# The second tile's attention in quarter steps, and a new order of eight loops: an RWKV-6 and GELU MLP kernel

## Chip, cores and metric

One core of a Trainium2 chip. The metric is the device time of one execution in microseconds (us), the median of three runs. An engine's own time is read from one profiled execution, whose span runs from its first instruction to its last.

## What is computed

The reference, cut to what matters (batch B=4, heads H=8, sequence S=768, head width D=48; the MLP has 3072 rows, 384 columns, 2048 hidden columns):

```python
for t in range(S):
    cur = einsum('bhd,bhe->bhde', u[None] * k[t], v[t])
    y[:, :, t] = einsum('bhd,bhde->bhe', r[t], state + cur)
    state = w[t][..., None] * state + einsum('bhd,bhe->bhde', k[t], v[t])
x = y.transpose(0, 2, 1, 3).reshape(B * S, H * D)
h = x @ w_in
out = (0.5 * h * (1 + erf(h / sqrt(2)))) @ w_out
```

So a linear attention with a decay w per key column and a bonus u for the current step, followed by a GELU MLP over its rows. All data are float32, the weights of the MLP arrive as float64.

## The kernel before

**Tiles and loops.** The 3072 rows are cut into eight tiles of 384 (a half sequence of one batch, all heads). `for x in range(NX)` (L1241) runs eight loops. Loop x interleaves the MLP of tile x-1 (`mlp`, L920) with the attention of tile x (`attention`, L373) and the first steps of the attention of tile x+1. In loop 0 there is no MLP: two halves of tile 0's attention run beside each other. After the last loop comes the MLP of tile 7 alone. The "second tile" is tile 1, whose attention lies in loop 1 (the second loop); the third tile's loop is loop 2.

**Order.** Each part is a Python generator that emits a few instructions and yields. `PLAN[x]` (L38) is a string, one character per step: `.` the MLP (in loop 0 the first half of tile 0's attention), `s` the current tile's attention, `f` the next tile's, `l` loads of the next tile, `c` conversion of weights, `w` masks and sums of weights, `x` sums of x. Every engine takes its instructions in the order in which the strings emit them, and what a string leaves over is emitted at its end. The strings come from a planner with costs of its own, outside the kernel.

**Attention inside a tile.** Time is cut into chunks of 64. Inside a chunk the score matrix (`a_sb`) is built in levels. `halves` (L489) has six levels h = 1, 2, ..., 32: a block of 2h steps is cut in two, PE multiplies the keys of the chunk with the queries of the later halves (`products`, L465, 48 products of 64x64 by 32 columns for tile 1), DVE multiplies r and k in place by the decay across the half (L525), and DVE (L536, by mask) or ACT (L533, by rows, from h=16) copies the result out of PSUM into `a_sb`. `quarters` (L560), which tiles 2 to 7 use, takes steps of four blocks: h=4 covers what levels 4 and 8 do, h=16 what 16 and 32 do, with 48 products of 96 columns (L608). It needs the queries laid out with their decays (ACT L577, DVE L582 and L583), updates r (L662) and k (L669, L673), and copies out by mask on DVE (L641) or by rows on ACT (L624). Levels 1 and 2 of these tiles are done by `transposed_sums` on DVE (L398).

**State.** k is turned: tiles 0 and 1 do it on PE (L705) with a copy on ACT (L707); tiles 2 to 7 by DVE block transposes (L556), twelve DMAs of 32x32 blocks on SP's queue (`move_block`, L551) and four ACT copies (L715). Then come `kv_ps` (L731), the chain of states on DVE (L746), y inside a chunk (L772), y from the states (L817), and the copies to the MLP's input xT (L824, L840, L843 with small DMAs L847).

**Weights.** w_in and w_out are 16 pieces of 768 columns (0 to 7 w_in, 8 to 15 w_out), turned from float64 to float32 by three ACT and three DVE instructions each (`prepare` L350 to L352, `finish` L363, L365, L369). The buffers between ACT and DVE are two deep (`HALFWAY`), the raw ones five (`AHEAD`); the load of piece i+3 is emitted when piece i is finished (L335). `w_sums` (L858) makes three sums of quarters of w_out in eight subtractions (L864) for the MLPs from tile 1 on, which multiply 2x2 blocks with seven products instead of eight. The MLP of tile 0 uses the plain form (L1074, L1168: 16 row blocks of w_out, two products each).

**PSUM.** Up to loop 1 there are three pairs of banks (`pair`) and two single ones (`mm`); after it two pairs and two `u` banks (`fewer_pairs`).

Of the kernel before, what the change touches and what calls it, by code (L numbers as in the profile page):

```python
# [28 lines left out]
LEVELS = (1, 2, 4, 8, 16, 32)  # L29
QUARTERS = (4, 16)  # L30
FINE = 4
# [4 lines left out]
NC_SP = 8  # L36
HALFWAY = 2
PLAN = {  # L38
    0: ".lls.....sslsc.lsslll.sl.sls..sl.lscsl..sss.lscs.lscs.s.clll.s..s.cccsss...wss..ss.ff",
    1: (  # L40
        ".cswc.ccc.cccss.lc.ccscs..cc.cs.cclwcsc.ccssc.c.cccsccc..ssccc.c.lcls.cc.ccsc.w.clwscclccc"
        ".c.swcw.ss.ccs.lcsc..cwcccslccslff..w..fw.wfs..f..flffffffww"
    ),
    2: (
        "...l...s..ws.swssswssss.sslsw...ssss.sssws.ll..ws.w..lw.sw.wl.sls.sls..lf.s....sf..f.f.xx."
        "fxl.x.x"
    ),
    3: (
        "l..sss..s.s..s.s....s...s.ssllss.sss.s.s.ss.l..lsss..ssslss.ss.s..s......s..ls.llssf.sf.sf"
        "lf.f.x.x..xxfffxf"  # L50
    ),
    4: (
        "...s...lsl......s.s....sss..ssss..s..ss..s..s...llssslss....sl.sss...s...sll.sl.s.sfs..fsf"
        ".ff..xl.x.xfffxffx"
    ),
    5: (
        ".l..........ls.ss...s.sslls.ssss..ss.sls...sss..sssssl.ss.s..s.......s.lssll.sfsf.f.s.ff.x"
        "..x.xxxl"
    ),
    6: (  # L60
        "sss.sls.....s......ls.s....s.sssssss..s.....s.ss....s.s.ssss.s.l.ss.l.ls.l...s.l.lslssf.s."
        ".ffs..lff.xx..xffxffx"
    ),
    7: "......s.s....s.s...s.ssssss...sss.ss...sss..ssss.s...ss...s...s.s.ss.s.s.s.x.x...xxx",
}


# [5 lines left out]
def kernel(  # L73
# [232 lines left out]
            nc.gpsimd.tensor_copy(out=v, in_=ident[o, o].unsqueeze(1).to_broadcast([32, FINE, 32]))  # L306

    def make_quarter_masks():
        make_fine()
        yield  # L310
        for (h, a), m_q in m_qs.items():
            nc.vector.tensor_tensor(out=quarter[h][a], in0=s_qs[h][:, 0:m_q.shape[1]], in1=m_q, op=ALU.is_equal)
            yield
# [59 lines left out]
    def attention(x, unit):  # L373
# [114 lines left out]

        def halves():  # L489

            for h in LEVELS:
                m = C // 2 // h
                if np_ < NPART:

                    d = products(range(np_), lambda z, b, i, p: rc[z, b, i, p], C, h == 1)
                    d = d.rearrange("p g (n m two j) -> p g n m two j", two=2, j=h, m=m)[:, :, :, :, 1, :]
                else:
                    right = rc.rearrange("p b i c (m two j) -> p b i c m two j", two=2, j=h)[:, :, :, :, :, 1, :]
                    d = products(range(np_), lambda z, b, i, p: right[z, b, i, p], C // 2)
                    d = d.rearrange("p g (n m j) -> p g n m j", j=h, m=m)  # L500
                if h == 1:
                    yield
                    diag = diagonal()
                yield

                r2 = r.rearrange("p (n two j) -> p n two j", two=2, j=h)[:, :, 1, :]
                t2 = tot[h].rearrange("p (n two) -> p n two", two=2)[:, :, 0:1].to_broadcast(r2.shape)
                k2 = k.rearrange("p (n two j) -> p n two j", two=2, j=h)[:, :, 0, :]
                tk = tot[h].rearrange("p (n two) -> p n two", two=2)[:, :, 1:2].to_broadcast(k2.shape)
                rk = bass.AP(tensor=r2.tensor, offset=r2.offset, ap=[r2.ap[0], [n_u - h, 2]] + list(r2.ap[1:]))  # L510
                tt = bass.AP(tensor=t2.tensor, offset=t2.offset, ap=[t2.ap[0], [1, 2]] + list(t2.ap[1:]))

                def update(z, r2=r2, t2=t2, k2=k2, tk=tk):
                    nc.vector.tensor_mul(*((k2, k2, tk) if z is k else (r2, r2, t2)))

                if x == 0 and m == 1:

                    update(k)
                    last_r.append(lambda: update(r))
                elif x == 0 and h == 1:  # L520
                    update(r)
                    yield
                    update(k)
                else:
                    nc.vector.tensor_mul(rk, rk, tt)  # L525
                yield
                ah = at.rearrange("p g n (m two j) -> p g n m two j", two=2, j=h)[:, :, :, :, 1, :]
                if h >= 16:

                    for p in range(2):  # L530
                        for i in range(m):
                            s = slice(p * 64 + i * 2 * h, p * 64 + i * 2 * h + h)
                            nc.scalar.copy(out=ah[s, :, :, i], in_=d[s, :, :, i])  # L533
                else:
                    mask = masks[h].rearrange("p (m j) -> p m j", j=h).unsqueeze(1).unsqueeze(1)
                    nc.vector.copy_predicated(out=ah, mask=mask.to_broadcast(ah.shape), data=d)  # L536
                if h == 1:
                    copy_diagonal(diag)
                yield
# [20 lines left out]
        def quarters():  # L560
# [28 lines left out]
            for h in QUARTERS:  # L589
                m, r4, t4, s0, s1, s2 = views(h)  # L590

                def burst(first, behind, spare=False):

                    d = [bank_u(i) for i in range(2)] if spare else pair("d")
                    if behind == n_b and h == FINE:
                        for a in range(FINE):
                            for g in range(2):
                                for p in range(2):
                                    nc.tensor.matmul(fine_of(d, g)[half[p], a * n_b:],  # L599
                                                     lhsT=places[half[g], a, p * C:(p + 1) * C],  # L600
                                                     rhs=fine_sb[half[g], 0:FINE - a, a],
                                                     start=(a == 0), stop=True, skip_group_check=True)
# [39 lines left out]
                        o += w_q  # L642

                last = h == QUARTERS[-1]
                whole = last and x % 2 == 0
                cuts = (0, n_b // 3, 2 * n_b // 3, n_b) if whole else (0, 5, 10, n_b)
                parts_of = list(zip(cuts, cuts[1:]))
                ds = [burst(*parts_of[0])]
# [1 line left out]
                    yield  # L650
                ds.append(burst(*parts_of[1]))
                if whole:
                    ds.append(burst(*parts_of[2], spare=True))
                yield
                copy_quarters(*parts_of[0], ds[0])
                yield
# [26 lines left out]
                for z, d in list(zip(parts_of, ds))[1:]:  # L683
                    copy_quarters(*z, d)
                    yield
                if h == FINE:
                    mask = fine_mask.rearrange("p (m b) -> p m b", b=FINE).unsqueeze(1)
                    for g in range(2):
                        data = fine_of(ds[-1], g).rearrange("p (b n) -> p n b", n=n_b)
# [3 lines left out]
                        yield  # L693

        last_r = []
        yield from halves() if x < 2 else quarters()


        if x < 2:
            kts = []  # L700
            for b in range(np_):
                kt_ps = pair("kt_ps")
# [523 lines left out]
    def next_v():  # L1226
        load_v(1, nc.sync)
        yield

    def warm():  # L1230
        for _ in range(2):
            keep_warm(3, True)
            yield

    def masks_and_sums():
        yield from make_quarter_masks()
        yield from w_sums()

    pieces_of_w = weights()
    slots = iter(())  # L1240
    for x in range(NX):  # L1241
# [8 lines left out]
        else:  # L1250
# [1 line left out]
                ".": mlp(x - 1), "s": slots, "f": following,  # L1252
                "l": load(x + 1, nc.sync),
                "x": sums_of_x(x) if x > 1 else iter(()),
                "w": masks_and_sums() if x == 1 else chain(first_sum(), h_sums()) if x == 2 else iter(()),
                "c": pieces_of_w if x == 1 else iter(()),
            }
        for c in PLAN[x]:
# [69 lines left out]
```

## Time and profile before

| What | us |
|---|---|
| Median of three runs (lowest, highest) | 593.21 (592.66, 593.95) |
| The profiled execution, its own time | 593.38 |
| Its span | 591.6 |
| PE busy in the span | 573.7 |
| DVE busy | 453.5 |
| ACT busy | 279.8 |
| First MLP product of tile 0 (L1074) | at 46.0 |
| End of tile 0's w_out products and of tile 1's y (L817) | at 114.8 |
| First MLP product of tile 2 (L949) | at 193.2 |

The profile has, for each instruction, its engine, line, tile names, start and length. A float32 matmul of the program is two records on PE. A wait is put down to what ended last before it. The chain of work is followed back from the last instruction; the table of stretches gives the busy time of each engine in a window.

### The profile page before, as it was taken

How to read it: one execution, taken by the hardware profiler on the slowest of the kernel's cores; microseconds unless marked ns; L12 is line 12 of the kernel's file. 1: busy time of each engine (PE TensorE's matmuls, PEld its weight loads, DVE VectorE, ACT ScalarE, POOL GpSimd, SP SyncE). 2: the span in 40 equal slices, each digit the busy share in tenths (PEclk: the TensorE clock that was granted, in tenths of full speed). 3: DMA queues.
4: the chain of work that ended last, by engine and by line, in shares of the span. 5: the costliest groups of instructions: out<-in, count | busy, mean ns of one | idle time of the engine just before them, and what ended most of it. 6: DMA issues, size and time to landing. Idle time of an engine off the chain costs nothing.

```text
span 591.6 us, 17422 instructions
## 1 busy us (share of the span) xinstructions
PE 573.7 (97%) x7522; PEld 510.8 (86%) x7536; DVE 453.5 (77%) x871; ACT 279.8 (47%) x648; POOL 8.0 (1%) x21
## 2 busy tenths in 40 slices
PE   5779999999999999999999999999999999999998
PEld 3566666766799999999999999999999999999997
DVE  5989989998969986787859987688859998421432
ACT  2367889223612558046462458145560465435400
POOL 3100000000000000000000000000000000000000
DMA  6658581020142302241032311330025200210000
GB/s 237 197 192 308 163 287 56 32 89 2 29 140 78 108 22 35 76 125 38 1 61 84 122 38 21 93 120 2 2 34 160 72 2 8 35 46 0 1 14 33
DMA packets 51004, 46.80 MB, mean 79 GB/s; under 512 B 31728, under 2 KB 36080, under 8 KB 50928
## 3 DMA queue, kind: packets, MB, share of 16 engines
q1 hardware_dynamic: 50832, 45.62, 25.6%
q8 instruction: 59, 0.97, 0.7%
q14 instruction: 17, 0.14, 0.1%
q10 hardware_dynamic: 96, 0.07, 0.1%
HBM read 36.24 MB, written 4.72 MB: 69 GB/s over the span
## 4 chain that ended last, share of the span: by engine, by line
PE 91%; DVE 3%; DMA 2%; issue 1%; ACT 1%; SPq 0%; DVEq 0%; ACTq 0%
PE o_ps L1088 33%; PE h_ps L949 16%; PE u_ps L949 14%; PE h_ps L1074 11%; PE d L608 4%; PE o_ps L1168 4%; PE d L472 2%; PE y_ps L772 2%; PE y_ps L817 2%; PE kv_ps L731 2%; DVE st L746 1%; DMA rkw<-in_rkw_dram 1%; DMA raw<-in_w_in_dram 1%; ACT a_sb L533 1%; PE d L599 1%
## 5 line engine op out<-in xcount | busy, mean ns | idle before, releaser
L949 PE MATMUL h_ps<-xT,w_in_sb 128*128 128x192 f32 x480 | 95.5, 330 | 0.4 <-DVE o_sb L1185 0.4
L949 PEld LDWEIGHTS h_ps<-xT,w_in_sb 128*128 128x128 f32 x480 | 79.7, 190 | 4.0 <-ACT g L981 1.5
L1074 PE MATMUL h_ps<-xT,w_in_sb 128*128 128x384 f32 x192 | 64.2, 490 | 0.1
L1074 PEld LDWEIGHTS h_ps<-xT,w_in_sb 128*128 128x128 f32 x192 | 35.8, 190 | 24.1 <-ACT xT L824 0.4
L1088 PE MATMUL o_ps<-w_out_sb,g 128*128 128x192 f32 x224 | 39.7, 326 | 0.0
L1088 PEld LDWEIGHTS o_ps<-w_out_sb,g 128*128 128x128 f32 x224 | 37.0, 190 | 0.3
L949 PE MATMUL u_ps<-s,w_in_sb 128*128 128x192 f32 x192 | 35.3, 327 | 0.0
L624 ACT COPY a_sb<-d 32x256 f32<-32x256 f32 (+8 forms) x90 | 32.6, 363 | 4.6 <-PE d L608 3.1
L472 PEld LDWEIGHTS d<-rkw 64*64 64x64 f32 x1152 | 19.5, 138 | 15.6 <-issue 10.0
L949 PEld LDWEIGHTS u_ps<-s,w_in_sb 128*128 128x128 f32 x192 | 31.7, 190 | 0.2
L1088 PE MATMUL o_ps<-w_out_sb,f 128*128 128x192 f32 x176 | 31.6, 329 | 0.0
L1088 PE MATMUL o_ps<-t,g 128*128 128x192 f32 x176 | 31.4, 329 | 0.0
L1088 PE MATMUL o_ps<-w_out_sb,e 128*128 128x192 f32 x176 | 31.4, 329 | 0.0
L1088 PE MATMUL o_ps<-t,e 128*128 128x192 f32 x176 | 31.2, 328 | 0.0
L1088 PE MATMUL o_ps<-t,s 128*128 128x192 f32 x176 | 30.9, 327 | 0.0
L746 DVE SCALAR_TENSOR_TENSOR st<-st,tot_sb,kv_ps 128x48 f32<-128x48 f32 x160 | 29.0, 258 | 1.7 <-PE kv_ps L731 1.6
L472 PE MATMUL d<-rkw 64*64 64x64 f32 (+1 forms) x1152 | 22.1, 225 | 8.1 <-DMA rkw<-in_rkw_dram 4.1
L641 DVE COPY_PREDICATED a_sb<-quarter,d 128x480 f32<-128x480 uint8 (+5 forms) x54 | 23.2, 438 | 8.6 <-PE d L608 7.3
L1088 PEld LDWEIGHTS o_ps<-t,g 128*128 128x128 f32 x176 | 28.7, 190 | 0.4
L1088 PEld LDWEIGHTS o_ps<-w_out_sb,e 128*128 128x128 f32 x176 | 28.7, 190 | 0.3
L1088 PEld LDWEIGHTS o_ps<-w_out_sb,f 128*128 128x128 f32 x176 | 28.7, 190 | 0.3
L1088 PEld LDWEIGHTS o_ps<-t,e 128*128 128x128 f32 x176 | 28.8, 190 | 0.2
(165 smaller groups left out, 1134.0 us busy)
## 6 DMA issues: line engine op xcount, KB each, us to landing
rkw<-in_rkw_dram SPq DMA_DIRECT2D x54, 256.0 KB, 3.8
raw<-in_w_out_dram SPq DMA_DIRECT2D x8, 768.0 KB, 4.4
v_in<-in_v_dram SPq DMA_DIRECT2D x8, 584.0 KB, 3.9
raw<-in_w_in_dram SPq DMA_DIRECT2D x5, 768.0 KB, 7.0
out_dram<-o_sb SPq DMA_DIRECT2D x20, 192.0 KB, 2.0
rkw<-kx SPq DMA_DIRECT2D x72, 48.0 KB, 2.1
rkw<-in_rkw_dram SPq DMA_DIRECT2D x6, 384.0 KB, 5.5
raw<-in_w_in_dram SPq DMA_DIRECT2D x9, 256.0 KB, 5.1
```

The costliest lines, as they stand in the source:

```text
L472: nc.tensor.matmul(d[half[p], g, n * width:(n + 1) * width], lhsT=kc[half[g], b, i, p], rhs=right(half[g], b, i, p), start=True, stop=True)
L608: nc.tensor.matmul(o[half[p], i * 3 * C // 2:(i + 1) * 3 * C // 2], lhsT=kc[half[g], n // NI, n % NI, p], rhs=rx[half[g], 2 * n + p], star ...
L624: nc.scalar.copy(out=at[z, g, first:behind, (a + 1) * h:], in_=d[z, :, :, to] if g == slice(None) else d[z, :, to])
L641: nc.vector.copy_predicated(out=an[:, :, :, :, (a + 1) * h:], mask=mask.to_broadcast(data.shape), data=data)
L731: nc.tensor.matmul(kv_ps[half[g], p, i * D:(i + 1) * D], lhsT=k_t(b, i, p, g), rhs=vs(b, i, g)[half[p], 0:D], start=True, stop=True)
L746: nc.vector.scalar_tensor_tensor(out=stq[:, q, c], in0=stq[:, q, c - 1] if c else b4[:, q, NC - 1], scalar=totq[:, q, c:c + 1], in1=kvs[q ...
L772: nc.tensor.matmul(y[p][half[g ^ swap(b)], i * C:(i + 1) * C], lhsT=vs(b, i, g)[half[p]], rhs=at[half[p], g, b * NI + i, :], start=(i == 0 ...
L817: nc.tensor.matmul(ys[b][0][c % 2][half[g ^ swap(b)], i * C:(i + 1) * C], lhsT=src[half[g], o:o + G], rhs=rc[half[g], b, i, c % 2], start= ...
L949: nc.tensor.matmul(o, lhsT=lhsT, rhs=rhs, start=start, stop=True, skip_group_check=True)
L1074: nc.tensor.matmul(h_ps, lhsT=w_in_sb[:, f // FI, j, f % FI * 128:(f % FI + 1) * 128], rhs=xT[:, j, :], start=(j == 0), stop=(j == NJ - 1))
L1088: nc.tensor.matmul(o, lhsT=lhs(j), rhs=rhs(j), start=start and j == 0, stop=(j == HF - 1), skip_group_check=True)
L1168: nc.tensor.matmul(o, lhsT=block(i, f // HF, f % HF), rhs=w_out_sb[:, f, :], start=(f == 0), stop=(f == NF - 1))
```

## The change

- Tile 1's attention does levels 1 and 2 by `halves` and the rest by `quarters` (steps 4 and 16), each step in three parts of four blocks, all on pairs of banks; the fine step of `quarters` stays with tiles 2 to 7. Its k is turned as in tiles 2 to 7 (DVE transposes, twelve DMAs on SP, four ACT copies).
- The quarter masks are made in loop 0 (behind the load of tile 1's v) instead of loop 1; the fine mask stays in loop 1.
- `w_sums` is one generator shared by two loops: four of its eight steps in loop 1, the rest in loop 2.
- All eight strings of `PLAN` are new.

```diff
 PLAN = {
-    0: ".lls.....sslsc.lsslll.sl.sls..sl.lscsl..sss.lscs.lscs.s.clll.s..s.cccsss...wss..ss.ff",
+    0: ".ll.s.s...slls.ssscll.lll..ss.ll.ss.lssl.ssclsc.l.ssslc.ls..sc..s.ss..wwswwccc.ccss.s.ccs.",
     1: (
-        ".cswc.ccc.cccss.lc.ccscs..cc.cs.cclwcsc.ccssc.c.cccsccc..ssccc.c.lcls.cc.ccsc.w.clwscclccc"
-        ".c.swcw.ss.ccs.lcsc..cwcccslccslff..w..fw.wfs..f..flffffffww"
+        "cscss.c..cscsslcc.lsss.ccl.cls.ccscc.ccs.ls.ccs..cclssssscsc.ssswccss..cs.cc.scc.c.cc.cssc"
+        "c.ccc.lscc.c.cwcccclc.lsccccwcc.f..w...fw....f.fffffflf"
     ),
...
     def make_quarter_masks():
-        make_fine()
-        yield
         for (h, a), m_q in m_qs.items():
...
-            for h in LEVELS:
+            for h in LEVELS if x == 0 else LEVELS[:2]:
...
-                    if behind == n_b and h == FINE:
+                    if behind == n_b and h == FINE and x > 1:
...
-                whole = last and x % 2 == 0
+                whole = x == 1 or last and x % 2 == 0
...
-                    ds.append(burst(*parts_of[2], spare=True))
+                    ds.append(burst(*parts_of[2], spare=x > 1))
...
-                if h == FINE:
+                if h == FINE and x > 1:
...
-        yield from halves() if x < 2 else quarters()
-        if x < 2:
+        if x < 2:
+            yield from halves()
+        if x > 0:
+            yield from quarters()
+        if x == 0:
             kts = []
...
     def next_v():
         load_v(1, nc.sync)
         yield
+        yield from make_quarter_masks()
...
+    of_w_out = w_sums()
     def masks_and_sums():
-        yield from make_quarter_masks()
-        yield from w_sums()
+        make_fine()
+        yield
+        yield from islice(of_w_out, 4)
...
-                "w": masks_and_sums() if x == 1 else chain(first_sum(), h_sums()) if x == 2 else iter(()),
+                "w": masks_and_sums() if x == 1 else chain(of_w_out, first_sum(), h_sums()) if x == 2 else iter(()),
```

In the built program the lines behind the change stand one or two apart from before (L1168 is L1169, L731 is L732, L608 is L606, L556 is L554, L551 is L549). On PE, tile 1's 48 products with u now stand ahead of the first three row blocks of the MLP instead of behind the first; in loop 1 the steps are level 1, the products with u, nine MLP products, level 2, nine, step 4, eighteen, step 16, twelve, eight of w_out, kv, four of w_out, y, six, y from the states, fourteen. On DVE, weight pieces 0 and 1 and two thirds of piece 2 stand ahead of the copies to xT (before: piece 0 and two thirds of piece 1), pieces 0 to 10 ahead of the chain of states (before: pieces 0 to 14 and the first instruction of piece 15), and the last piece's last instruction after two sums instead of three. On SP, the twelve DMAs of tile 1 stand ahead of the loads of pieces 11 to 14.

## The prediction

> **What bounds the kernel now.** I read the busy shares first, then the table of stretches, then the chain in order of time, then each engine's timeline around the second loop (tile 0's MLP beside tile 1's attention), which the change rewrites. The busy shares:
>
> ```profile
> PE 573.7 (97%) x7522; PEld 510.8 (86%) x7536; DVE 453.5 (77%) x871; ACT 279.8 (47%) x648; POOL 8.0 (1%) x21
> ```
>
> PE is the bound on average. An average hides stages, so I took stretches of 15 us (columns: PE, PEld, DVE, ACT, POOL, clock, DMA share, GB/s):
>
> ```profile
> 45.00:60.00 15.00, 14.95 (x230) 9.40 (x229) 14.71 (x22) 11.77 (x24) 0.00 (x0) 1.00 0.86 302
> 60.00:75.00 15.00, 15.00 (x163) 9.10 (x163) 14.90 (x18) 12.84 (x24) 0.00 (x0) 1.00 0.54 168
> 75.00:90.00 15.00, 15.00 (x218) 9.73 (x211) 12.92 (x17) 12.86 (x22) 0.00 (x0) 1.00 0.76 274
> 90.00:105.00 15.00, 15.00 (x248) 9.91 (x250) 14.19 (x30) 13.07 (x18) 0.00 (x0) 1.00 0.17 55
> 105.00:120.00 15.00, 15.00 (x244) 11.85 (x237) 14.59 (x25) 4.49 (x10) 0.00 (x0) 1.00 0.12 37
> ```
>
> From 45 to 120 us PE never rests, but DVE is busy for 71.3 of 75 us and ACT for 50.6 of the first 60: a second and a third engine stand just under the bound. The chain, in order of time (start, length, what):
>
> ```profile
> 84.16 1.53 PE d L472 x96
> 85.69 7.94 PE o_ps L1168 x24
> ...
> 97.93 1.31 PE kt_ps L705 x12
> ...
> 100.54 1.54 PE kv_ps L731 x96
> ...
> 113.26 1.56 PE y_ps L817 x96
> 114.82 5.40 PE o_ps L1088 x32
> ```
>
> It is PE back to back, so a microsecond taken from PE counts only if DVE, ACT and SP deliver that much sooner. What they deliver, in the timelines (start, length):
>
> ```profile
> 89.87 0.55 DVE L363 TENSOR_SCALAR f<-f 128x768 uint32<-128x768 uint32 x1
> 90.34 0.95 DVE L365 SCALAR_TENSOR_TENSOR e<-raw,e 128x768 uint32<-128x768 uint32 x1
> 91.32 0.96 DVE L369 CUSTOM_DVE_ANT_0 w_out_sb<-f,e 128x1536 uint16<-128x1536 uint16 x1
> ...
> 102.31 3.58 DVE L746 SCALAR_TENSOR_TENSOR st<-st,tot_sb,kv_ps 128x48 f32<-128x48 f32 x20
> ...
> 106.79 0.96 DVE L369 CUSTOM_DVE_ANT_0 w_out_sb<-f,e 128x1536 uint16<-128x1536 uint16 x1
> ...
> 153.19 1.96 DVE L556 STREAM_TRANSPOSE kx<-rkw 128x384 f32<-128x384 f32 x4
> 155.30 8.87 SPq L551 DMA_DIRECT2D rkw<-kx  x12
> 166.14 1.61 PE L731 MATMUL kv_ps<-v_in,rkw 64*64 64x48 f32 x96
> ```
>
> One weight piece takes DVE 2.33 us start to start (89.87 to L864's start at 92.20); piece 15, the last, is done at 107.7, and PE needs it two row blocks of w_out (2 x 1.33, four records of 0.331 each) before 113.26, at 110.6: 2.9 us of slack. The last three lines are the third loop, where k is turned by DVE and moved by 12 DMAs: kv follows the transposes by 11.0 us (8.87 to issue, 2.1 to land). In the other loops this gap is 10.4 to 11.7.
>
> [...]
>
> **The change, part by part** (pieces counted from 0).
> PE, second loop: out go four levels (4 x 1.53) and 12 transposes (1.31), 7.4 us. In come two steps of 48 products of 96 columns; 40 records of that kind take 0.99 us in the chain, so 96 take 2.38, two steps 4.75. Net -2.7 us.
>
> DVE: out go four updates (1.75 each) and the masked copies of levels 4 and 8 (0.98 each), 9.0. In: per step a layout (0.56 + 0.96), an update of r (1.35), two of k (0.96 each), 9.6 for both; nine masked copies, 1.32 per part of four between the rows for 480/320/160 columns (0.69/0.50/0.33), 4.0; transposes 2.0. Net +6.6 in the stage where DVE had 2.9 to spare. Four of the eight sums go out (0.95 each, 3.8), but only one of them stood ahead of the last weight piece, so 0.9 helps PE's wait.
>
> ACT: out 1.90 + 1.59 + 1.50 = 5.0; in six plain copies 2.7, 18 row copies 6.8 (six take 2.28), four block copies 2.1. Net +6.5, beside 12.8 of 15 busy.
>
> SP: the 12 moves stand ahead of the loads of pieces 11 to 14, which wait behind them. The quarter masks (0.5) go to the first loop, where DVE idles 1.3 us before the first kv: nothing; if that cover is gone, 0.5.
>
> Start: PE now has all 48 diagonal products ahead of the first MLP matmul; they need ACT's u-scaling (2.13), and ACT has another weight preparation (2.8) before it. xT's last copy began at 44.60 when the ACT queue's DMAs were issued; I put u-scaling at 45.7 to 47.8, the diagonal's end at 49.0. Before, it ended at 49.74 with 1.98 of MLP done ahead of it, equal to 47.7: +1.3 us. Bounds 0 (ACT has the raw data early) to +2.
>
> **The queues added up.** DVE from the fences at 41.8 to the end of the transposes, in starts: six pieces 14.0, xT 2.2, totals 2.6, two updates 3.4, masked copies of levels 1 and 2 3.6, diagonal 1.8, layouts 3.0, r 2.6, k 3.8, quarter copies 4.0, transposes 1.9: 42.9, so 84.7. No wait in between: each product it reads is done by then. The moves are issued by 92.9 to 93.8, landed by 95.0 to 95.9: kv at 95.2. PE would be there at 49.0 + 5.96 + 1.53 + 5.96 + 2.38 + 11.9 + 2.38 + 7.94 + 5.3 = 92.4 (nine MLP products, level 2, nine, first step, eighteen, second step, twelve, then eight of w_out, in the order of the changed program, at 0.331 a record). So 2.8 us of stall (part of it already spent on piece 8, which DVE ends at 87.6 where PE asks at 87.1, and on gelu behind the row copies on ACT).
> Then kv ends at 96.75, the states chain 97.1 to 100.6, and only then comes piece 11: 102.9. PE, after kv, has two row blocks and y (2.65 + 1.75) to 101.15, and waits to 103.2: 2.0 more. From there it has ten row blocks (13.25) and y's second half (1.56): 118.0. DVE's rest (five pieces, two sums, fences, 13.5) ends at 114.1, in time for the last 2.65. Before: 114.8. Loop two is +3.2 (1.3 - 2.7 + 2.8 + 2.0, less 0.2 of rounding).
>
> Third loop: DVE comes 6 us later into tile 2's attention, but has its own waits for PE there, and PE's first burst stands 2 us later; transposes then end near 161, kv near 171.3, PE there at 171.2: 0 to +0.8, I take 0.4. Loops four to eight do the same work in another order; before has about 1.3 us of PE idle time from 240 to 480, so a new plan can gain that at most, and I allow the same as loss: 0.
> Sum on the profiled execution: 593.4 (span 591.6 and 1.8 around it) + 3.6 = 597.0; the median of the runs is 0.2 lower: 596.8.
>
> **Rivals.**
> (A) The above, +2 to +6: chance 0.60.
> (B) PE stays dense: faster. It decides if kv is ready when PE comes, that is if the transposes end by 82 instead of 84.7 and pieces 11 to 15 stay ahead. Then 1.3 - 2.7 = -1.4: 591.8; with the start not late, 590.5. For it: DVE overlaps starts, and the sums could leave it shorter. Against: 42.9 us of DVE in 42.9 us. 0.20.
> (C) Stalls and gain cancel, within 0.2% (1.2 us, about what a measurement can tell from no change): the moves come sooner and piece 11 is not late, 593 to 594.4: 0.08.
> (D) ACT falls behind as well: weight buffers are two deep, so each late gelu or row copy delays a preparation, DVE waits for it, and the third loop's kv is late too: +6 to +8, 600. For it: ACT 85% busy before the +6.5. 0.12.
>
> Slower is A and D, 0.72; same 0.08; faster 0.20. The range 591.2 to 599.3 leaves out D and a little of B. A's own range is 595.2 to 599.3.
>
> **What would show it.** PE idle ahead of kv (L732) and ahead of the L1169 block after y, 1 to 3 us each, with DVE or DMA as the releaser; transposes L554 ending at 84 to 86; the last w_out piece near 114 instead of 107.7; L1089's first start near 118 instead of 114.8; from there the loops of equal length. Wrong if PE shows 15.00 in every stretch to 120 and L1089 starts by 113.5, or if the difference lies after 200 us.

## The result, and the profile after

The changed kernel takes 599.41 us (median of four runs, 596.92 to 600.05), the kernel before beside it on the same chip 593.58 (592.66 to 594.41): ratio 1.0085, 95% interval 1.0062 to 1.0107. The execution that was profiled took 600.05, with a span of 598.2 (before 591.6). The busy shares of the changed kernel:

```profile
PE 574.4 (96%) x7318; PEld 509.3 (85%) x7332; DVE 458.7 (77%) x888; ACT 285.6 (48%) x668; POOL 8.0 (1%) x21
```

The averages look as before: PE +0.7 us, DVE +5.3, ACT +5.8. The stretches of 15 us show the place (columns as before: PE, PEld, DVE, ACT, POOL, granted clock, DMA share, GB/s):

```profile
45.00:60.00 15.00, 11.84 (x236) 7.86 (x229) 11.67 (x16) 7.47 (x15) 0.00 (x0) 0.89 0.93 326
60.00:75.00 15.00, 15.00 (x136) 9.27 (x135) 14.79 (x19) 11.78 (x26) 0.00 (x0) 1.00 0.35 123
75.00:90.00 15.00, 14.11 (x132) 8.38 (x131) 14.62 (x27) 13.81 (x34) 0.00 (x0) 1.00 0.07 11
90.00:105.00 15.00, 12.56 (x220) 7.74 (x218) 10.13 (x30) 11.03 (x19) 0.00 (x0) 0.99 0.75 239
105.00:120.00 15.00, 14.95 (x132) 9.14 (x133) 14.60 (x21) 11.88 (x17) 0.00 (x0) 0.90 0.33 119
```

PE was busy for 14.95 or more in each of the five before. Now it rests clearly in three of them, and in two its clock is 0.89 to 0.90. The two stretches with the longest rests are those with the fullest DMA engines (0.93 and 0.75). That alone explains nothing: before had 0.86 and 0.76 in two of its stretches, with PE busy for 14.95 and 15.00. In between, DVE is full. PE's timeline of the changed kernel (start, length, what, and in brackets the idle time ahead of it and what ended it; "issue" is time in which PE waited for nothing that the profile shows):

```profile
45.16 0.55 PE L470 MATMUL d<-kx,rkw 64*64 64x64 f32 x23
48.87 1.28 PE L470 MATMUL d<-kx,rkw 64*64 64x64 f32 x73 [3.16 <-issue]
50.08 7.75 PE L1075 MATMUL h_ps<-xT,w_in_sb 128*128 128x384 f32 x18
57.77 1.60 PE L470 MATMUL d<-rkw 64*64 64x32 f32 x96
59.30 6.07 PE L1075 MATMUL h_ps<-xT,w_in_sb 128*128 128x384 f32 x18
...
102.86 0.93 PE L773 MATMUL y_ps<-a_sb,v_in 64*64 64x64 f32 x47 [0.93 <-issue]
105.05 5.64 PE L1169 MATMUL o_ps<-w_out_sb,g 128*128 128x384 f32 x12 [1.27 <-DVE w_out_sb L367]
```

Three things are to be seen. In the middle of the products with u, after 23 of 96 records, PE stops for 3.16 us. The nine MLP products after that take 7.75 us, the same nine ten microseconds later 6.07: the clock. The same pair comes again at 103 to 105 us: two rests, and then 5.64 us for six products that take 4.14 where the clock is full (e12). The changed kernel in stretches of 3.41 us, around both places:

```profile
46.68:50.09 3.41, 1.22 (x74) 1.15 (x73) 2.61 (x7) 2.72 (x3) 0.00 (x0) 1.00 0.97 293
50.09:53.50 3.41, 3.41 (x11) 1.90 (x7) 3.18 (x3) 0.00 (x0) 0.00 (x0) 0.50 1.03 375
...
101.29:104.71 3.42, 1.56 (x89) 1.28 (x80) 2.38 (x5) 3.36 (x4) 0.00 (x0) 1.00 1.03 411
104.71:108.12 3.41, 3.07 (x5) 1.85 (x6) 3.11 (x7) 3.34 (x5) 0.00 (x0) 0.50 1.04 393
```

At both places PE's clock was at half for 3.41 us, and the two stretches start 54.6 us apart, 16 times 3.41. In the 3.41 us ahead of each, PE was idle for 2.19 and 1.86 us, so not throughout. What decides is worked out at the end.

From L1089's first start, at 121.40 (before 114.75), to the end of the span it is 476.8 us in both kernels. So all of the loss lies ahead of that point. I call the stage from the first start of y from the states (L818, L817 before) in loop 0 to the first start of L1089 (L1088 before) "the stage": 74.76 us before, 82.23 after. (It starts 0.82 us sooner than before, so L1089 starts 6.65 us later.) The account of these 7.5 us, from PE's timeline:

| Term | us |
|---|---|
| Rest in the products with u ("issue") | +3.16 |
| Rest inside y (L773, "issue") | +0.93 |
| Three waits for gelu behind ACT's row copies (0.39, 0.51, 0.29) | +1.19 |
| Wait for a w_out piece ahead of L1169 | +1.27 |
| Low clock: 7.75 - 6.07 and 5.64 - 4.14 | +3.2 |
| Less work of PE (not measured: what is left of 7.47) | -2.3 |

### The profile page after: what moved, and what is told of

Its sections match the earlier page's. It is cut to its first block, busy times and chain, and to the rows that moved or that the text cites. A ratio compares the mean times of both kernels' runs of the same rounds, so it can differ in the third digit from the quotient of the medians.

```text
span 598.2 us, 17069 instructions
## 1 busy us (share of the span) xinstructions
PE 574.4 (96%) x7318; PEld 509.3 (85%) x7332; DVE 458.7 (77%) x888; ACT 285.6 (48%) x668; POOL 8.0 (1%) x21
## 4 chain that ended last, share of the span: by engine, by line
PE 87%; ACT 5%; DVE 3%; issue 2%; DMA 1%; SPq 0%; DVEq 0%; ACTq 0%
PE o_ps L1089 32%; PE h_ps L950 16%; PE u_ps L950 13%; PE h_ps L1075 10%; PE d L606 5%; PE o_ps L1169 3%; ACT a_sb L622 2%; PE kv_ps L732 2%; PE y_ps L818 2%; PE y_ps L773 2%; PE d L470 1%; DVE st L747 1%; DMA rkw<-in_rkw_dram 1%; ACT a_sb L531 1%; ACT rkw L716 1%
## 5 line engine op out<-in xcount | busy, mean ns | idle before, releaser
L1075 PE MATMUL h_ps<-xT,w_in_sb 128*128 128x384 f32 x192 | 66.3, 501 | 0.9 <-ACT rkw L1080 0.9
L1075 PEld LDWEIGHTS h_ps<-xT,w_in_sb 128*128 128x128 f32 x192 | 36.5, 194 | 26.9 <-ACT rkw L1080 2.6
L622 ACT COPY a_sb<-d 32x256 f32<-32x256 f32 (+8 forms) x108 | 39.1, 362 | 5.9 <-PE d L606 4.1
L1089 PE MATMUL o_ps<-w_out_sb,g 128*128 128x192 f32 x224 | 39.7, 326 | 0.0
L1089 PEld LDWEIGHTS o_ps<-w_out_sb,g 128*128 128x128 f32 x224 | 37.0, 190 | 0.3
L639 DVE COPY_PREDICATED a_sb<-quarter,d 128x480 f32<-128x480 uint8 (+7 forms) x63 | 27.1, 439 | 10.4 <-PE d L606 8.9
L606 PEld LDWEIGHTS d<-kx,rkw 64*64 64x64 f32 x1248 | 27.2, 133 | 7.2 <-issue 5.1
L606 PE MATMUL d<-kx,rkw 64*64 64x96 f32 x1248 | 32.7, 247 | 0.2 <-ACT a_sb L622 0.2
L1089 PE MATMUL o_ps<-w_out_sb,f 128*128 128x192 f32 x176 | 31.7, 330 | 0.0
L1089 PE MATMUL o_ps<-w_out_sb,e 128*128 128x192 f32 x176 | 31.4, 329 | 0.0
L1089 PE MATMUL o_ps<-t,s 128*128 128x192 f32 x176 | 31.2, 328 | 0.0
L1089 PE MATMUL o_ps<-t,g 128*128 128x192 f32 x176 | 31.0, 328 | 0.0
L1089 PE MATMUL o_ps<-t,e 128*128 128x192 f32 x176 | 30.9, 327 | 0.0
L1078 ACT ACTIVATE g<-h_ps 128x256 f32<-128x256 f32 (+1 forms) x32 | 14.0, 436 | 35.4 <-PE h_ps L1075 35.3
L1089 PEld LDWEIGHTS o_ps<-t,g 128*128 128x128 f32 x176 | 28.7, 190 | 0.3
L1089 PEld LDWEIGHTS o_ps<-w_out_sb,e 128*128 128x128 f32 x176 | 28.7, 190 | 0.3
L1089 PEld LDWEIGHTS o_ps<-t,s 128*128 128x128 f32 x176 | 28.8, 190 | 0.2
```

Source lines behind the costliest of these rows:

```text
L606: nc.tensor.matmul(o[half[p], i * 3 * C // 2:(i + 1) * 3 * C // 2], lhsT=kc[half[g], n // NI, n % NI, p], rhs=rx[half[g], 2 * n + p], star ...
L622: nc.scalar.copy(out=at[z, g, first:behind, (a + 1) * h:], in_=d[z, :, :, to] if g == slice(None) else d[z, :, to])
L639: nc.vector.copy_predicated(out=an[:, :, :, :, (a + 1) * h:], mask=mask.to_broadcast(data.shape), data=data)
L1075: nc.tensor.matmul(h_ps, lhsT=w_in_sb[:, f // FI, j, f % FI * 128:(f % FI + 1) * 128], rhs=xT[:, j, :], start=(j == 0), stop=(j == NJ - 1))
L1078: nc.scalar.activation(out=gs[group][:, f % FG, 0:t], in_=h_ps[:, 0:t], func=AF.Gelu)
L1089: nc.tensor.matmul(o, lhsT=lhs(j), rhs=rhs(j), start=start and j == 0, stop=(j == HF - 1), skip_group_check=True)
```

## Experiments

The kernel before, run beside them, had medians of 594.1 to 594.7. "Stage" is that of the one profiled execution, and the waits are PE's in it. The executions of one kernel differ by 1.4 to 8.3 us, in most kernels along with PE's mean clock. For the kernel with the load behind xT, three took 596.7 to 597.1 us with a mean clock of 0.994 to 0.997, and three 599.3 to 600.4 with 0.991 (one stretch of 3.41 us at half clock is 1.7 us, or 0.003 of 597). So a stage shows where the time goes in one execution, and the ratio what it is worth.

| Run | Median, us | Ratio (95%) | Stage | Waits: issue / ACT / DVE | Clock in the stage |
|---|---|---|---|---|---|
| before | 593.58 | 1 | 74.8 | 0 / 0 / 0.5 | 1.00 |
| changed | 599.41 | 1.0085 (1.0062 to 1.0107) | 82.2 | 4.1 / 1.2 / 1.8 | 0.96 |
| e1 | 601.33 | 1.0111 (1.0083 to 1.0138) | 84.0 | 1.5 / 1.3 / 5.4 | 0.96 |
| e2 | 600.18 | 1.0089 (1.0061 to 1.0117) | 77.9 | 1.7 / 1.2 / 2.0 | 1.00 |
| e3 | 600.67 | 1.0107 (1.0072 to 1.0143) | 83.1 | 3.5 / 1.2 / 1.3 | 0.98 |
| e4 | 616.20 | 1.0361 (1.0321 to 1.0401) | 79.8 | 3.0 / 1.2 / 1.9 | 0.98 |
| e5 | 598.19 | 1.0082 (1.0050 to 1.0113) | 79.1 | 2.3 / 3.0 / 1.0 | 1.00 |
| e6 | 598.48 | 1.0074 (1.0050 to 1.0098) | 79.3 | 1.1 / 3.2 / 2.1 | 1.00 |
| e7 | 598.76 | 1.0085 (1.0060 to 1.0110) | 79.5 | 0 / 3.1 / 1.5 | 0.98 |
| e8 | 600.89 | 1.0101 (1.0069 to 1.0132) | 82.6 | 5.0 / 1.2 / 2.0 | 0.96 |
| e9 | 599.90 | 1.0092 (1.0059 to 1.0125) | 82.5 | 6.9 / 0 / 1.1 (DMA 0.9) | 0.98 |
| e10 | 605.34 | 1.0185 (1.0155 to 1.0215) | 86.5 | 0 / 4.0 / 3.7 | 0.92 |
| e11 | 602.44 | 1.0144 (1.0108 to 1.0180) | 84.4 | 0 / 0.6 / 3.7 (DMA 3.4) | 0.94 |
| e12 | 597.35 | 1.0060 (1.0026 to 1.0094) | 77.8 | 2.0 / 2.1 / 0.7 | 1.00 |

**e1: the first MLP row block ahead of the products with u.**

```diff
-        "cscss.c..cscsslcc.lsss.ccl.cls.ccscc.ccs.ls.ccs..cclssssscsc.ssswccss..cs.cc.scc.c.cc.cssc"
+        "cscs.sc..cscsslcc.lsss.ccl.cls.ccscc.ccs.ls.ccs..cclssssscsc.ssswccss..cs.cc.scc.c.cc.cssc"
```

> One character of the second loop's string is moved: the first MLP row block (three products) stands ahead of tile 1's 48 products with u again, as in the kernel before. Theory (the late start is a real loss, and the rest of PE that it causes also lowers PE's clock): PE has no gap of 1.28 us in the middle of those products, the clock stays at 1.00 after 50 us, L1089 starts 2 to 3 us sooner than 121.4, and the time is 596.5 to 597.5. Rival (PE waits for the late weight pieces and for kv in any case, so that a better start is given back): kv and L1089 start where they did, 599 to 600.

(The gap meant is the one of 3.16 us; 1.28 us is the length of the run of products behind it.) It was not faster, and the mechanism was wrong. PE's timeline of this run:

```profile
49.16 4.18 PE L1075 MATMUL h_ps<-xT,w_in_sb 128*128 128x384 f32 x6 [3.20 <-DVE f L361]
```

The row block now stood in front and waited 3.20 us itself. DVE's L361, which it is put down to, doesn't write what this product reads. Its inputs are xT and a piece of w_in that was done at 33.3. The small moves into xT were issued from 42.09 on and took 7.0 us to land (median), so till about 49.1: that is what ended the wait. The DMA list of the kernel before for 30 to 60 us (size, median us from issue to landing) has:

```profile
xT<-ysb SPq DMA_DIRECT2D x3, 24.0 KB, 3.0
```

The same list of the changed kernel has:

```profile
xT<-ysb SPq DMA_DIRECT2D x3, 24.0 KB, 6.7
```

And that of e1:

```profile
xT<-ysb SPq DMA_DIRECT2D x3, 24.0 KB, 7.0
```

So the start is late for a reason in loop 0, not because of the products with u alone. In the changed kernel too the xT moves landed only at 48.1 and later (41.43 + 6.7). Without its rest PE would have come to the first MLP product at about 47 and waited there: the rest of 3.16 us and the late landing lie over each other. On SP's queue the changed kernel issues v's load (584 KB, at 39.43), then the load of weight piece 4 (768 KB, at 39.82), and then the xT moves (41.43). Before had v's load at 40.25, the xT moves at 42.29 and the piece's load after them, at 44.20. The piece's load belongs to a conversion step: the new string of loop 0 has twelve such steps instead of eight.

**e3: PE kept busy in the rest** (adds work that no one reads, in front of each half of the products with u).

```diff
+            if x == 1 and rest:
+                for _ in range(6):
+                    nc.tensor.matmul(d[:, 0], lhsT=zeros[:, 0:128], rhs=zeros, start=True, stop=True)
```

> Twelve products of zeros (128 x 512, bf16) that no one reads are added on PE ahead of tile 1's 48 products with u, in the 3.2 us in which PE rested at 45 to 50 us; nothing is taken away. Theory (the drop of PE's clock to 0.5 to 0.6 at 50 to 54 us comes from that rest): the clock stays at 1.00, the first nine MLP products take 5.96 us instead of 7.75, and the time falls by 1 to 1.7 us, to 597.7 to 598.5. Rivals: the drop has another cause (clock still 0.5 to 0.6, time 599.4 or more); or it is given back at kv (clock 1.00, L1089 still at 121.4, 599.4).

The clock was 1.00 from 45 to 60 us, and the nine products took 6.07 us. That is as the theory has it: with less idle time (1.80 us in a window of 3.41 us, against 2.19 in the changed kernel) there was no drop. But no time was gained: PE still stopped for 2.30 us ("issue"), and the added products take 2.9 us of their own. The stop now came after 18 records instead of 23, with six added products ahead of it (24 against 23): here its place follows the count of instructions, not the product. A second drop (0.89 in 105 to 120) came as in the changed kernel.

**e5: the load of piece 4 behind the xT moves.** Four conversion steps go from the end of loop 0 back into loop 1.

```diff
-    0: ".ll.s.s...slls.ssscll.lll..ss.ll.ss.lssl.ssclsc.l.ssslc.ls..sc..s.ss..wwswwccc.ccss.s.ccs.",
+    0: ".ll.s.s...slls.ssscll.lll..ss.ll.ss.lssl.ssclsc.l.ssslc.ls..sc..s.ss..wwswwccc.ss.s.s.",
...
-        "cscss.c..cscsslcc.lsss.ccl.cls.ccscc.ccs.ls.ccs..cclssssscsc.ssswccss..cs.cc.scc.c.cc.cssc"
+        "cscccccss.c..cscsslcc.lsss.ccl.cls.ccscc.ccs.ls.ccs..cclssssscsc.ssswccss..cs.cc.scc.c.cc.cssc"
```

> Four conversion steps are moved from the end of loop 0 to the start of loop 1, as in the kernel before, so that the load of weight piece 4 (768 KB) stands behind the small moves into xT on SP's queue instead of ahead of them; the order of PE stays changed. Theory (the new order of loop 0 puts that load in front, the xT moves then land in 6.4 to 7.0 us instead of 3.0, and PE's gap of 3.2 us with the low clock behind it follows from that full DMA stretch): xT moves land in 3 to 4 us, the gap shrinks below 1 us, the clock stays 1.00, the first MLP product starts at 47 to 48 instead of 50.1, and the time is 595 to 597.5. Rival (the gap comes from the 48 products with u standing in front, whatever the loads do): gap and start as they were, 599 to 600.5.

In the trace the theory holds for the start. The xT moves on SP's queue landed in 2.3 us. The products with u were still in front, yet the rest was 0.16 us. PE's timeline of this run:

```profile
46.02 1.32 PE L470 MATMUL d<-kx,rkw 64*64 64x64 f32 x73 [0.16 <-issue]
47.27 4.14 PE L1075 MATMUL h_ps<-xT,w_in_sb 128*128 128x384 f32 x12
53.11 2.20 PE L1075 MATMUL h_ps<-xT,w_in_sb 128*128 128x384 f32 x6 [1.70 <-ACT rkw L1080]
...
102.12 0.93 PE L773 MATMUL y_ps<-a_sb,v_in 64*64 64x64 f32 x48 [2.09 <-issue]
```

The MLP starts at 47.27 instead of 50.08, and the clock stays at 1.00. But 1.70 us of the gain went at once into a wait for gelu, which stands behind two weight preparations on ACT, and the rest inside y was 2.09 us, not 0.93. The stage is 3.1 us shorter; the ratio, 1.0082, can't be told from the changed kernel's.

What is the "issue" rest? The DMA list has a queue "instruction". In steps of half a microsecond, it shows when a packet of it is moved. The changed kernel, 46.0 to 46.5 (packets, MB, share of 16 engines):

```profile
q8 instruction: 1, 0.02, 14.9%
```

The same queue in e5, 43.5 to 44.0:

```profile
q8 instruction: 1, 0.02, 12.0%
```

In all runs whose products with u are in front, PE goes on 2.2 to 2.8 us after the start of this packet:

| Run | Packet moved in | PE goes on at | Rest |
|---|---|---|---|
| e5 | 43.5 to 44.0 | 46.02 | 0.16 |
| e4 | 44.0 to 44.5 | 46.81 | 2.06 |
| e12 | 44.5 to 45.0 | 47.49 | 1.07 |
| e2 | 46.0 to 46.5 | 48.57 | 1.69 |
| changed | 46.0 to 46.5 | 48.87 | 3.16 |
| e3 | 47.5 to 48.0 | 50.24 | 2.30 |
| e8 | 47.5 to 48.0 | 50.16 | 4.02 |
| e9 | 47.5 to 48.0 | 50.16 | 4.26 |

It is the same inside y: packet in 100.5 to 101.0, PE on at 102.86 (changed); 99.5 to 100.0 and 102.12 (e5); 102.5 to 103.0 and 105.39 (e9). The queue's packets are of 16 KB (58 with 0.95 MB in the changed kernel). That PE rests because it waits for instructions in such a packet is my reading of the queue's name and of these times; no view shows it. In the changed kernel's execution three of those from 30 us on stand ahead of a rest and the others don't, so a packet alone makes none. But of the 32 "issue" rests that the fourteen traces have from 30 us on, all but one (0.34 us in e9) end 2.2 to 2.8 us after the start of a packet, and in seven of the eight runs of the table the stop comes after the same 23 records. The kernel before has such a rest too, in tile 0's `kv_ps`. Its packet was moved in 36.5 to 37.0 us:

```profile
q8 instruction: 1, 0.02, 11.7%
```

PE goes on at 39.23, and while it rests the DMA engines have almost nothing to do (a share of 0.02):

```profile
39.23 0.20 PE L731 MATMUL kv_ps<-v_in,kx 64*64 64x48 f32 x1 [1.10 <-issue]
```

```profile
38.10:39.20 1.10, 0.02 (x3) 0.00 (x0) 0.97 (x7) 0.09 (x1) 0.00 (x0) 1.00 0.02 7
```

All fourteen traces show that one (0.99 to 1.95 us). So full DMA engines aren't needed for such a rest. That they lengthen it is argued from one pair: in e5, where PE has the same order and is only 0.15 us later, the packet was moved 2.6 us sooner than in the changed kernel, and the rest was 3.0 us shorter. What the packet itself waited for is not recorded; that it stood behind load packets is argued from the order of the loads and from e5.

**e6: the start in all as before** (e5 and e1 together; the edit is shown against e5).

```diff
-        "cscccccss.c..cscsslcc.lsss.ccl.cls.ccscc.ccs.ls.ccs..cclssssscsc.ssswccss..cs.cc.scc.c.cc.cssc"
+        "cscccccs.sc..cscsslcc.lsss.ccl.cls.ccscc.ccs.ls.ccs..cclssssscsc.ssswccss..cs.cc.scc.c.cc.cssc"
```

> As the last one, and the first MLP row block stands ahead of the 48 products with u. Theory (the row block alone did not help since its input xT had not landed; with the load behind, it has): the first MLP product at 46 to 47, no gap over 1 us up to 80 us, L1089 at 117 to 118.5, the time 595 to 597. Rival (the stage is set by DVE and ACT from 50 us on, so that an earlier start is given back ahead of kv): L1089 at 120 to 121.5, 598.5 to 600.

The first MLP product starts at 46.72 and there is no rest in the products with u, but a wait of 1.81 us for gelu follows. L1089 starts at 119.93, in a run whose loop 0 ended 1.45 us later than the changed kernel's: a stage of 79.3, as e5. The median, 598.5, is the rival's: an early start is given back later.

**e2: k turned on PE again.**

```diff
+                elif x == 1:
+                    yield
...
-        if x == 0:
+        if x < 2:
             kts = []
```

> Tile 1's k is turned on PE again, as in the kernel before: no block transposes on DVE, no twelve moves on SP, no four block copies on ACT; the quarter steps stay. Theory (the moves hold back kv and the loads of weight pieces 11 to 14): PE gets 1.3 us more work, kv (L732) starts 3 to 4 us sooner than 96.6, the wait ahead of w_out after y (1.27 us with a low clock after it) goes, L1089 at about 118: 595.5 to 597. Rival (DVE's and ACT's longer queues alone make the pieces late): L1089 not before 120.5, 598.5 to 600.

No rest inside y any more. Without the moves the loads are done sooner (from 98.5 to 106 us the DMA engines' share is 0.16 or less, in the changed kernel 0.96 or more), but the twelve products added on PE also go with a packet at another place (94.0 to 94.5, ahead of kv); this run doesn't tell the two apart. L1089 starts at 118.11, as the theory has it, but in the fastest of the six executions (597.19), in which PE's clock never dropped in the stage. And kv starts at 95.96 instead of 96.63, not 3 to 4 us sooner, and the wait ahead of w_out stays (1.35). DVE's timeline of this run shows why:

```profile
90.70 0.56 DVE L361 TENSOR_SCALAR f<-f 128x768 uint32<-128x768 uint32 x1 [3.02 <-ACT f L348]
```

The preparation of piece 10 stands on ACT behind three blocks of row copies (2.26 to 2.28 each, from 78.38 to 89.32) and four gelus. Where the moves no longer hold back the pieces, ACT does. The theory's time fails: ratio 1.0089.

**e7: start as before and k on PE.** The edits of e6 and e2.

> As the last one, and tile 1's k is turned on PE again. What is left of the change are the quarter steps, the split of the sums and the order of the later loops. Theory (start and moves are two losses that add): L1089 at 114.5 to 116, the time 592.5 to 594.5. Rival (ACT's row copies of the second step hold back the preparation of the pieces, and DVE with them, in either form): L1089 at 117 to 118, 595.5 to 597.

The rests are gone from the stage (issue 0), and ACT and DVE waits of 4.7 us stand in their place: 1.82 for gelu behind the preparations, 1.1 behind the row copies, 1.36 for a w_out piece that waited for ACT. The clock of 0.98 comes from ahead of the stage: the rest in tile 0's `kv_ps` took 1.95 us here, and half clock followed from 42.0 to 45.5. The two losses don't add; the rival's mechanism is seen, its time missed by 2.

**e9: the second step's row copies left out.**

```diff
+                    if m == 1 and x == 1:
+                        return
                     if m == 1:
                         copy_rows(first, behind, d, slice(None))
```

> Part of the work is left out: the 18 row copies on ACT (6.8 us) that bring the second quarter step of tile 1 out of PSUM. All else is as in the changed kernel. Theory (ACT is a second-order cause: gelus and the preparation of pieces 9 and 10 wait behind these copies, but kv waits for the moves, which do not need ACT): PE's three waits for gelu (0.3 to 0.5 us each at 86 to 92) go, kv starts within 0.5 us of 96.6, the time falls by 0 to 1: 598.4 to 599.4. Rival (ACT is the bound of the stage): kv and piece 11 come 3 us sooner, 595.5 to 597.

PE has no wait for ACT in the stage, and kv now waits for the moves (0.86 us). The time is 599.9, so 6.8 us less of ACT gained nothing. But the two "issue" rests took 4.26 and 2.30 us in this execution, 2.5 us more than in the changed kernel, so what the copies cost by themselves is not separated. PE reached kv at 96.33, and the moves, of which the last had landed 0.2 us ahead of kv in the changed kernel, then became the last.

**e8: all eight sums in loop 1.**

```diff
-        "c.ccc.lscc.c.cwcccclc.lsccccwcc.f..w...fw....f.fffffflf"
+        "c.ccc.lscc.c.cwcccclc.lsccccwcc.f..www...fwww....f.fffffflf"
...
-        yield from islice(of_w_out, 4)
+        yield from islice(of_w_out, 8)
```

(In loop 2's string the first four `w` are taken out.)

> The changed kernel with all eight sums of w_out in the second loop, behind the last weight pieces, and none in the third: the split of the sums is undone, the rest stays changed. Theory (only sums ahead of the last piece hold back PE, and these come behind it): within 0.6 us of the changed kernel, 599 to 600; PE's idle time in the third loop as it was. Rival (DVE, with 2 to 4 us more at 110 to 125 us, is late with the third tile's attention): 1.5 to 3 us more, 601 to 602.5.

L1089 starts at 121.98, and 477.2 us follow (476.8 in the changed kernel). The interval covers the changed kernel's ratio: the split of the sums is worth nothing that can be measured.

**e4: the strings of loops 3 to 7 from the kernel before.**

> The strings of loops 3 to 7 are those of the kernel before; loops 0 to 2 stay changed. Theory (all of the loss lies ahead of 121 us): 599.4, give or take 0.6. Rival (the new order of the later loops costs by itself): 595 to 597.

Both expectations fail, since the experiment was not what I took it for. Loop 2's new string takes six steps of the next tile, the old one five, so the old string of loop 3 meets another step than it was planned for. PE's waits from 211 to 277 us then add up to over 12 us, and two stretches of 6.83 us at half clock come with them (6.8 us more); of the 19.4 us that follow L1089 beyond the changed kernel's 476.8, that is nearly all. One line of PE's timeline of this run:

```profile
248.68 0.42 PE L732 MATMUL kv_ps<-v_in,rkw 64*64 64x48 f32 x2 [3.06 <-DMA rkw<-kx]
```

It tells nothing of the new order of the later loops. The equal 476.8 us do: their new order is worth nothing in sum. What it does tell is that a string can't be put back alone.

**e10: ACT's work in another order** (shown against e5): row blocks and gelus ahead of the preparations at the start, parts 1 and 2 of the row copies behind the last gelus and piece 10.

```diff
-        "cscccccss.c..cscsslcc.lsss.ccl.cls.ccscc.ccs.ls.ccs..cclssssscsc.ssswccss..cs.cc.scc.c.cc.cssc"
+        "css.sc.ccc.cccscsslcc.lsss.ccl.cls.ccscc.ccs.ls.ccs..cclssssscsc.ssswccs..c.csc.sscc.c.cc.cssc"
```

> Built on the run with the load behind the xT moves. In the second loop's string ACT's work is put in the order in which it is needed: the first row blocks and their gelus ahead of the preparation of pieces 3 and 4, and parts 1 and 2 of the second step's row copies behind the gelus of the last row blocks and the preparation of piece 10. No work is added or removed. Theory (after the start, PE's waits for gelu behind preparations and row copies, 1.7 + 1.3 us, are real losses): these waits go, the stage from the states' y of tile 0 (L818's first start) to L1089's first start falls from 79.1 to 76.5 to 77.5 us. Rival (they are given back in front of kv and the w_out pieces, which wait for the moves and the loads behind them): the stage stays at 78.5 to 79.5.

A clear miss, and slower than the rival too: the stage is 86.5. Of the 7.4 us over e5's stage most is the clock, which was at half for 6.83 us behind each of the two long waits below. The timelines of ACT and PE in this run:

```profile
96.31 4.54 ACT L622 COPY a_sb<-d 32x256 f32<-32x256 f32 x12
100.87 2.08 ACT L716 COPY rkw<-kx 32x384 f32<-32x384 f32 x4
...
101.95 0.86 PE L732 MATMUL kv_ps<-v_in,rkw 64*64 64x48 f32 x6 [3.39 <-ACT rkw L716]
```

The late gelus wait for PE (1.85 and 1.38 us of ACT's time), the row copies stand behind them, and the copies of the moved k (L716), which kv needs, behind those. In the changed kernel the row copies used time in which ACT had nothing else: the 1.2 us that PE waits for gelu is the price of an earlier kv. At the start a wait of 3.15 us for DVE's level-1 copies took the place of the wait for gelu, since more preparations stood ahead of them.

**e11: loads ahead of the moves** (shown against e10).

```diff
-        for _ in weight_in(i + 3):
-            pass
+        for j in range(i + (3 if i < 6 else 5), i + (4 if i < 5 else 6)):
+            for _ in weight_in(j):
+                pass
```

> As the last one, and the loads of weight pieces 9 to 15 are issued up to two pieces sooner (when the raw buffer is free), so that those of pieces 11 and 12 stand ahead of tile 1's twelve moves on SP's queue. Theory (behind the moves the loads pile up at 95 to 100 us: piece 11 is late, and PE's own wait of 1 to 2 us in y lies in that full DMA stretch): the wait ahead of L1169 after y goes, the one inside y shrinks below 1 us, the stage falls by a further 1.5 to 2.5 us, to 74.5 to 75.5, and the time comes within 0.3% of the kernel before. Rival (the chain of states stands ahead of piece 11 on DVE, whenever it is loaded): less than 0.7 us gained.

The stage is 2.1 us shorter than e10's, but up to 1.7 of that is the clock, which was at half for one stretch of 3.41 us less, and 84.4 is far from the theory's 74.5 to 75.5. On the loads the run is inconclusive, because kv waits for the copies of the moved k here as well (3.37 us), so late that the loads have landed in either order.

**e12: the pieces of this together**, with the changed kernel's row copies (shown against e5).

```diff
-        "cscccccss.c..cscsslcc.lsss.ccl.cls.ccscc.ccs.ls.ccs..cclssssscsc.ssswccss..cs.cc.scc.c.cc.cssc"
+        "csccccss..c.sscccslcc.lsss.ccl.cls.ccscc.ccs.ls.ccs..cclssssscsc.ssswccss..cs.cc.scc.c.cc.cssc"
...
-        for _ in weight_in(i + 3):
-            pass
+        for j in {5: (8, 9), 6: (10, 11), 7: (12,), 8: (), 9: ()}.get(i, (i + 3,)):
+            for _ in weight_in(j):
+                pass
```

> The changed kernel with the load of piece 4 behind the xT moves (four conversion steps moved into loop 1), the preparation of piece 4 behind the first two gelus on ACT, tile 1's first update and copies ahead of piece 3 on DVE, and the loads of pieces 9 to 12 one or two pieces sooner, so that those of 11 and 12 stand ahead of the twelve moves; those of 13 to 15 stay. The order of the row copies is the changed kernel's. No work is added or removed. Theory (what is left of the loss is PE's gaps where full DMA stretches meet the products with u and y, gelus behind preparations, and the late piece 11; not the sum of DVE's work): no PE gap over 1 us in the stage from L818's first start to L1089's first start, clock 1.00, the stage falls from 79.1 (load behind xT alone) to 75 to 76.5, as long as before's 74.8 within 2 us, and the time is 593.5 to 595.5. Rival (DVE's 6.6 us and the moves set kv and the pieces, so that any gap closed opens another in front of kv or w_out): the stage stays over 78, the time at 597 or more.

The time is the rival's (597 or more). The stage fits neither: 77.8 is longer than the theory's 75 to 76.5 and just below the rival's 78. PE's timeline:

```profile
47.49 1.32 PE L471 MATMUL d<-kx,rkw 64*64 64x64 f32 x73 [1.07 <-issue]
...
101.44 0.93 PE L774 MATMUL y_ps<-a_sb,v_in 64*64 64x64 f32 x48 [0.91 <-issue]
102.56 4.14 PE L1170 MATMUL o_ps<-w_out_sb,g 128*128 128x384 f32 x12 [0.20 <-DVE w_out_sb L368]
```

No rest is over 1.1 us, the stage's clock is 1.00, and piece 11 is nearly in time (0.20 instead of 1.27). The median, 597.35, is the lowest of the family; its interval ends at 1.0094, so even against the changed kernel it is no certain gain. Still 3.0 us over before's stage: 4.8 us of waits against 0.5, less 1.3 of PE's busy time. No version beats the kernel before.

## Why the prediction was right or wrong

The direction was right and the likeliest mechanism half right: PE does lose its density to the other engines and to DMA. The predicted 596.8 is 2.6 us short, and 599.41 lies just above the range. Against the kernel beside it the loss is 0.85%, or 5.0 us, where 3.6 were forecast. The sums of the prediction hold to 0.1 us; what failed is what they left out. Point by point:

- **PE -2.7.** Near: -2.3 is left in the account. A quarter step took 2.14 us from start to start (65.30 to 67.44), not 2.38.
- **DVE +6.6, ACT +6.5.** Right by durations: +6.7 and +6.1 in the whole program. Busy time, in which overlaps count once, rose by 5.3 and 5.8.
- **Transposes end at 84.7.** They end at 86.46, but not from DVE's queue, which I had put 1.3 us too long. DVE waited 0.86 and 2.23 us for PE at 50 and 59 us. "No wait in between: each product it reads is done by then" is the sentence that failed: PE had its rest and its low clock there.
- **kv at 95.2 after a stall of 2.8.** kv started at 96.63 and didn't wait. The moves were issued from 86.61 to 95.04, 1.2 to 2.1 us later than I had them, and PE itself came only at 96.6. (The time to issue twelve moves was not what failed: 8.0 to 8.9 us where the kernel before issues them in one go, L551, and 8.43 here.) e9 shows that the moves were close behind: with PE sooner, kv waits 0.86 us for them.
- **Piece 11 at 102.9, PE waits 2.0.** 105.0 and 1.27. The cause was as said (loads behind the moves, e12), with ACT's preparation, not DVE's chain, as the last link.
- **Start +1.3.** The diagonal's end came at 50.1 instead of 49.0, so the size was near, but the reason was wrong. I had ACT's u-scaling as the last thing, at 47.8. It was done at 46.5, and PE still rested to 48.87, put down to "issue" and 2.6 us behind the start of an instruction packet (46.27). On SP I counted tile 1's moves past the loads, and not the load of piece 4 past the xT moves, though my own text says that more of the conversion stands ahead of the copies to xT. A conversion's last step issues a load.
- **Later loops +0.4 and 0, sums nothing.** Right within its bounds: 476.8 us in both kernels, so the 0.4 didn't come; e8.
- **The term that was missing: the clock.** I counted PE in starts at full clock. Two drops, 3.2 us, turn a sum of +3.6 into about the +6.7 of the profiled execution (600.05 - 593.38); the other misses nearly cancel. That they do is luck: the stall of 2.8 us at kv, the largest term, didn't come, and a rest of 3.16 us that no term foresaw took its place.
- **Rival D** gave the right time, 600, for a wrong reason. ACT as the releaser of PE is 1.2 us of the stage, and there is no cascade into the third loop. **Rival B** failed at its point of decision, the transposes by 82.

Shown: where the loss lies, the landing of xT and its undoing (e5), the clock after rests (e3, e5, and the count at the end), and the tie in time between instruction packets and PE's rests. Argued only: that PE waits for such a packet, and what the packet waits for. Open: how much of the median each term makes up, since e2, e5, e6 and e7, each with a shorter stage in its profile, have ratios that can't be told from the changed kernel's. Not tested: the quarter steps alone. No run takes them out and keeps the new order, so what their load on DVE and ACT costs apart from the order is not known.

## What to carry to other kernels

When a step is moved, follow every DMA that it issues past what stands on its queue, and ask which small, urgent transfers (here the moves into xT, 6.7 us instead of 3.0, and perhaps the instruction packets) then share the DMA engines with a large load. On PE, price a rest with the clock behind it, not by its length alone: here the two stretches at half clock added 1.7 and 1.5 us. Rests that lie close together can count together: those of 0.93 and 1.27 us did. Where three engines are nearly full, a wait that is taken away is not a gain until the next one in line has been named: here gelu, L716 and the level-1 copies each took over in turn.

## What was not expected of the hardware

- PE rests for 0.2 to 4.3 us in the middle of a run of like products, and goes on 2.2 to 2.8 us after the start of a packet of 16 KB on the instruction queue (31 of the 32 rests from 30 us on). It does so with the DMA engines full (a share of 0.97 during the 3.16 us) and with them idle (0.02 during the 1.10 us).
- The length of a rest doesn't tell whether the clock drops: 2.06 us (e4) was followed by a drop, 2.09 us (e5) and 2.30 us (e3, e9) were not. In these traces what tells is PE's idle time within one window of 3.41 us. Every stretch at half clock here, but for those that the end of the run cuts off, is one or two such windows long, and in each run they all lie on one grid, which its first change of clock gives. Counted so in the thirteen traces other than before's, whose clock never changed, 24 windows at full clock had 1.84 us or more of PE idle time, and all 24 were followed by half clock; 1,049 had 1.81 us or less, and one was (1.56 us, in e8). Why that one was is open. PE's idle time is the window less PE's busy time as the profile has it. Some of these windows stand in the table below. The rest of 2.09 us in e5 is cut in two by the grid, and neither part is enough. Two rests of 0.93 and 1.27 us in the changed kernel fell for the most part into one window, and together they were enough.
- A move of 24 KB from SBUF to SBUF into xT landed in 1.9 to 4.3 us in the seven traces with the weight piece behind it, and in 5.3 to 7.9 us in the seven with one ahead of it.

| Run | Window, us | PE idle in it, us | Clock in the next |
|---|---|---|---|
| changed | 46.68 to 50.09 | 2.19 | 0.50 |
| e4 | 43.29 to 46.70 | 1.95 | 0.50 |
| changed | 101.29 to 104.71 | 1.86 | 0.50 |
| e6 | 52.42 to 55.84 | 1.81 | 1.00 |
| e3 | 48.49 to 51.90 | 1.80 | 1.00 |
| e5 | 97.77 to 101.18 | 1.15 | 1.00 |
| e5 | 101.18 to 104.59 | 1.25 | 1.00 |
